# Storing the last output tile with one transfer per queue and column half instead of two

## The chip, the cores and the metric

The kernel runs on one core of a Trainium2 chip. The core has a matrix engine (PE in the profile, with PEld for its weight loads), a vector engine (DVE), a scalar engine (ACT), GpSimd (POOL) and a sync engine (SP). SP, ACT and POOL can each issue transfers to and from HBM; all of these transfers are carried out by the core's 16 DMA engines. The metric is the device time of the whole program in microseconds, as the median over runs. The median before the change is 307.31 us (three runs, 307.09 to 307.4).

## The reference

The reference computes an attention with global and local tokens and feeds its result to a two-layer network. Only the end of the second part matters here:

```python
x = attn_out.transpose(0, 2, 1, 3).reshape(B * S, H * D)   # 8 * 544 = 4352 rows of 512
h = x @ w_in                                               # 512 -> 2048
g = h * (1.0 / (1.0 + np.exp(-1.702 * h)))
return (g @ w_out).astype(np.float32)                      # 2048 -> 512
```

B is 8 (batches), S is 544 rows in each batch: Sg = 32 global rows first and 512 local rows after them. The output is 4352 rows of 512 float32 numbers, so a row is 2,048 bytes.

## The kernel before

The attention of batch i + 1 is computed between the matrix products of batch i, so that the matrix engine always has work; the order is written out by hand. The network works on nine groups of rows: group i < 8 holds the 512 local rows of batch i, and group 8 (`i == B`) holds the 256 global rows of all batches. For each group, `h_step` makes 16 slices of the hidden layer (matrix products at L495, a tanh on ACT at L502, a product on DVE at L503), and `o_mm` then multiplies them with `w_out` for one tile of 128 output rows at a time (L520). A finished tile goes to `o_out` (L525 to L542): ACT copies it out of the accumulator into the buffer `ob` and scales it by 0.5 (L534), and four transfers store it in HBM (L542), each of 32 rows.

The group of global rows comes last, and it has two tiles of 128 rows. Each of them belongs to four batches: rows 32j to 32j + 31 of a tile are the 32 global rows of one batch, so in the output the four pieces stand 544 rows apart. The very last tile (`last` in L527) is treated on its own. Its columns are cut in two halves, 0 to 319 and 320 to 511. For each of them the matrix engine runs 16 products (L532), ACT evicts the half (L534), and four transfers of 32 rows store it, two issued by SP (j = 0 and 2) and two by ACT (j = 1 and 3). So the tile ends in eight transfers. All other output tiles are stored by SP alone.

The issues of a queue are made one after the other by its engine. On SP, the store of the tile before (four of 32 rows of 512 columns) stands directly ahead of the last tile's. On ACT, the two issues of the first half stand between the eviction of the first half and that of the second. Each transfer reports its landing on one of eight semaphores that are used in turn, and the program's end, on SP, waits for all of them (L824).

Of the kernel before, what the change touches and what calls it, by code (L numbers as in the profile page):

```python
# [20 lines left out]
def kernel(  # L21
# [12 lines left out]
    nc = tc.nc  # L34

    B, H, Sl, D = q_l.shape
    Sg = q_g.shape[2]
    S = Sg + Sl
# [105 lines left out]
    for i in range(2):  # L144
# [4 lines left out]
        out=step, in_=step, pattern=[[1, 257]], compare_op=ALU.is_ge,  # L149
# [89 lines left out]
    def pbank(name):  # L239
        return psP.tile([128, 512], F32, name=name, tag="p")  # L240
# [272 lines left out]
    def o_mm(i, st):  # L513
        tci, f4 = divmod(st, 4)
        first = (i, tci) not in ops
        if first:
            ops[i, tci] = pbank("op")
        op = ops[i, tci]
        for fc in range(4 * f4, 4 * f4 + 4):
            nc.tensor.matmul(op, lhsT=gTs[i][:, fc, tci * 128 : tci * 128 + 128],  # L520
                             rhs=w_out_sb[:, fc, :], start=(first and fc == 4 * f4), stop=(fc == FC - 1))
        if f4 == 3:
            o_out(i, tci, op)

    def o_out(i, tci, op):  # L525
        ob = moe.tile([128, d_model], F32, name="ob", bufs=6)
        last = i == B and tci == B // 4 - 1  # L527
        for lo, hi in ((0, 320), (320, 512)) if last else ((0, 512),):
            if last:
                op = pbank("op")  # L530
                for fc in range(FC):
                    nc.tensor.matmul(op[:, lo:hi], lhsT=gTs[i][:, fc, tci * 128 : tci * 128 + 128],  # L532
                                     rhs=w_out_sb[:, fc, lo:hi], start=(fc == 0), stop=(fc == FC - 1))
            nc.scalar.activation(ob[:, lo:hi], op[:, lo:hi], AF.Copy, scale=0.5)  # L534
            for j in range(4):
                eng = nc.scalar if last and j % 2 else nc.sync
                if i < B:
                    rows = out[i * S + Sg : (i + 1) * S, :].rearrange("(r t) m -> t r m", t=16)[4 * tci + j]
                else:
                    r = (4 * tci + j) * S  # L540
                    rows = out[r : r + Sg, :]
                eng.dma_start(out=rows[:, lo:hi], in_=ob[32 * j : 32 * j + 32, lo:hi])  # L542
# [253 lines left out]
    for st in range(4):  # L796
        o_mm(B, st)
    o_out(B, 1, None)


# [28 lines left out]
```

## Time and profile before

| What | us |
|---|---|
| median of the runs | 307.31 |
| span of the profiled execution | 305.3 |
| PE busy in it | 298.7 (98%) |
| last matrix products (L532), start and length | 298.06, 3.66 |
| eviction of the first half (L534), start and length | 300.43, 0.44 |
| eviction of the second half (L534), start and length | 301.80, 0.33 |
| ACT's two issues of the second half, start and length together | 302.16, 0.85 |
| issue to landing of the last tile's eight stores | 1.4 to 1.7 |

The profiled execution's own time outside of its span isn't listed. The median of the runs stands 2.0 us above the span; that is what lies around the span of instructions, in so far as the profiled execution was like the others.

Times in the profile's views are counted from the first instruction of the program. A name ending in q (SPq, ACTq) is an engine's issue of a transfer or its wait; its length is the time that the engine was held by the issue, not the time of the transfer. In the view of the transfers (the DMA view) a strip of 40 digits divides the stretch asked for into equal slices; a digit is the mean busy share of the 16 DMA engines in tenths, and below it stand the GB/s that they moved. q1 is the queue that SP issues to and q10 the one that ACT issues to.

### The profile page before, as it was taken

Reading aid. Unit: us, or ns where it says so; the run is one execution under the profiler, and the core shown is the slowest. Engines: PE = TensorE matmul, PEld = TensorE weight load, DVE = VectorE, ACT = ScalarE, POOL = GpSimd, SP = SyncE. Lnnn points to the kernel's source line nnn. Section 1 sums busy time; section 2 is a strip of 40 time slices with the busy share of each in tenths; the row PEclk is TensorE's granted clock in tenths of the full one; section 3 lists DMA queues with packets and bytes.
Section 4 is the critical chain, followed back from the end, with each engine's and each line's share of the span. In section 5 each row is a group of like instructions: output and inputs, shape, how many; then the busy total and the mean of one; then the engine's idle time right before and its main releaser. Section 6 shows DMA issues by size and latency. Waiting matters only on the chain.

```text
span 305.3 us, 7862 instructions
## 1 busy us (share of the span) xinstructions
PE 298.7 (98%) x3265; PEld 148.5 (49%) x3265; DVE 211.2 (69%) x445; ACT 169.3 (55%) x282; POOL 55.7 (18%) x89
## 2 busy tenths in 40 slices
PE   7999999999999999999999999999999999999995
PEld 6454445445454455445454455445454454446653
DVE  6678858978868876777767876787677855573320
ACT  4738484585556655575457654665456661673421
POOL 8732755530050002300050002100000000000000
PEclk9999999999999999999999999999999999999999
DMA  7999999999399023941299024901130021101122
GB/s 191 178 206 207 197 180 230 211 170 131 82 112 191 10 56 84 151 97 37 54 122 170 4 56 89 101 0 48 44 86 2 2 66 48 46 0 36 36 63 75
DMA packets 56436, 29.52 MB, mean 97 GB/s; under 512 B 43088, under 2 KB 46288, under 8 KB 56400
## 3 DMA queue, kind: packets, MB, share of 16 engines
q0 software_dynamic: 46000, 16.98, 49.9%
q1 hardware_dynamic: 9920, 11.39, 14.3%
q10 hardware_dynamic: 480, 0.66, 0.7%
q8 instruction: 25, 0.41, 0.6%
q14 instruction: 11, 0.09, 0.1%
HBM read 35.13 MB, written 8.91 MB: 144 GB/s over the span
## 4 chain that ended last, share of the span: by engine, by line
PE 80%; DMA 15%; DVE 2%; POOL 1%; issue 1%; ACT 0%; ACTq 0%; DVEq 0%; POOLq 0%
PE op L520 34%; PE hp L495 33%; DMA rk<-in_k_l_dram 10%; PE s L314 5%; PE ov L426 4%; DMA rq<-in_q_l_dram 3%; DMA w_in_sb<-in_moe_w_in_dram 2%; PE ov L400 2%; DVE xL L459 1%; PE op L532 1%; PE s L444 1%; PE s L333 1%; ACTq L542 0%; ACT ob L534 0%; DVE e L354 0%
## 5 line engine op out<-in xcount | busy, mean ns | idle before, releaser
L520 PE MATMUL op<-w_out_sb,gT 128*128 128x512 bf16 x528 | 122.0, 380 | 0.0
L503 DVE SCALAR_TENSOR_TENSOR gT<-th,hp 128x512 bf16<-128x512 f32 (+1 forms) x140 | 91.2, 657 | 41.8 <-ACT th L502 40.7
L495 PE MATMUL hp<-xL,w_in_sb 128*128 128x512 bf16 x496 | 108.9, 379 | 0.3 <-DVE xL L459 0.2
L502 ACT ACTIVATE th<-hp 128x512 f32<-128x512 f32 (+1 forms) x140 | 79.9, 573 | 43.4 <-PE hp L495 39.9
L495 PEld LDWEIGHTS <-w_in_sb 128*128 128x128 bf16 x576 | 56.2, 98 | 64.7 <-issue 0.9
L520 PEld LDWEIGHTS <-gT 128*128 128x128 bf16 x528 | 49.2, 98 | 56.2 <-issue 3.5
L347 ACT ACTIVATE e<-s 128x856 bf16<-128x856 f32 x62 | 51.6, 884 | 12.1 <-PE s L444 7.0
L534 ACT ACTIVATE ob<-op 128x512 f32<-128x512 f32 (+2 forms) x35 | 20.5, 585 | 59.0 <-PE op L520 56.5
L89 POOL DMA_DIRECT2D v<-in_v_l_dram x24 | 18.7, 782 | 111.2 <-PE s L444 105.8
L450 DVE STREAM_TRANSPOSE sT<-ov 128x512 f32<-128x512 f32 x15 | 10.8, 717 | 26.9 <-PE ov L426 26.9
L354 DVE TENSOR_TENSOR e<-e,mask 128x1408 bf16<-128x1408 bf16 x28 | 24.4, 872 | 5.7 <-ACT e L347 5.7
L314 PE MATMUL s<-q,kT 32*128 32x228 bf16 (+5 forms) x528 | 21.2, 280 | 1.0 <-DVE q L275 1.0
L459 DVE TENSOR_TENSOR xL<-ov,rs 128x512 bf16<-128x512 f32 x30 | 19.3, 686 | 1.4
L314 PEld LDWEIGHTS <-kT 32*128 32x128 bf16 x528 | 10.9, 95 | 14.8 <-issue 6.6
L271 DVE STREAM_TRANSPOSE kT<-rk 128x512 f32<-128x512 f32 (+1 forms) x17 | 16.9, 994 | 1.0 <-DMA rk<-in_k_l_dram 1.0
L383 ACT ACTIVATE ek<-kb 128x512 bf16<-128x512 f32 x16 | 9.7, 608 | 9.2 <-PE kb L333 7.0
L426 PE MATMUL ov<-e,v 128*32 128x160 bf16 (+1 forms) x480 | 12.2, 239 | 0.0
L454 DVE STREAM_TRANSPOSE rs<-rT 128x512 f32<-128x512 f32 x16 | 11.4, 711 | 0.6
L275 DVE STREAM_TRANSPOSE q<-rq 128x512 f32<-128x512 f32 (+1 forms) x17 | 10.9, 641 | 1.0 <-ACT rq L558 1.0
L426 PEld LDWEIGHTS <-v 128*32 128x32 bf16 x512 | 10.0, 97 | 0.9 <-issue 0.9
L333 PE MATMUL kb<-q,kgT 32*32 32x512 bf16 x128 | 10.4, 387 | 0.0
L495 PE MATMUL hp<-xG,w_in_sb 128*128 128x256 bf16 x64 | 9.6, 273 | 0.0
(82 smaller groups left out, 170.6 us busy)
## 6 DMA issues: line engine op xcount, KB each, us to landing
out_dram<-ob SPq DMA_DIRECT2D x132, 64.0 KB, 1.7
v<-in_v_l_dram POOLq DMA_DIRECT2D x32, 128.0 KB, 6.0
rk<-in_k_l_dram POOLq DMA_DIRECT2D x6, 512.0 KB, 10.8
rq<-in_q_l_dram POOLq DMA_DIRECT2D x5, 512.0 KB, 8.6
w_out_sb<-in_moe_w_out_dram POOLq DMA_DIRECT2D x4, 512.0 KB, 10.8
rq<-in_q_l_dram POOLq DMA_DIRECT2D x5, 256.0 KB, 8.9
ek<-ek SPq DMA_DIRECT2D x13, 96.0 KB, 2.9
w_in_sb<-in_moe_w_in_dram POOLq DMA_DIRECT2D x4, 256.0 KB, 6.4
```

The lines of the kernel that those rows point to most:

```text
L89: nc.gpsimd.dma_start(out=vtiles[b % 2][p, s, :, :, :D], in_=vf[b, g][:, hs])
L271: nc.vector.transpose(self.kT.rearrange("p (r t) -> p t r", t=16)[:, lo:hi], loaded[self.b][0][:, self.u].bitcast(F32)[:, 32 * lo : 32 * hi])
L314: nc.tensor.matmul(ps[j][:, off : off + n], lhsT=self.k[p, 128 * c : 128 * c + 128, e], rhs=self.q[p, lo:hi, r0 : r0 + nr, e], start=(e == ...
L347: nc.scalar.activation(e[:, 2 * i : 2 * i + 2, :RW], self.ps[i][:, :, :RW], AF.Exp, scale=scale)
L354: nc.vector.tensor_mul(e, e, mask[:, rnd : rnd + 1, :].to_broadcast([128, 4, LW]))
L426: nc.tensor.matmul(ov[32 * j : 32 * j + 32, :].rearrange("p (t r) -> p t r", t=16)[:, :, r0 : r0 + nr], lhsT=lv, rhs=self.E[c // 2][:, j, ...
L459: nc.vector.tensor_mul(self.x[:, 2 * self.u + h, :], self.st[1 + h], self.st["rs"])
L495: nc.tensor.matmul(hp[:, : width(i)], lhsT=w_in_c[:, fc // 8, kc, fc % 8 // 2, :, fc % 2], rhs=(xL[i] if i < B else xG)[:, kc, :], start=( ...
L502: nc.scalar.activation(th[:, :n], hp[:, :n], AF.Tanh, scale=0.851)
L503: nc.vector.scalar_tensor_tensor(gTs[i][:, fc, :n], in0=th[:, :n], scalar=1.0, in1=hp[:, :n], op0=ALU.add, op1=ALU.mult)
L520: nc.tensor.matmul(op, lhsT=gTs[i][:, fc, tci * 128 : tci * 128 + 128], rhs=w_out_sb[:, fc, :], start=(first and fc == 4 * f4), stop=(fc = ...
L534: nc.scalar.activation(ob[:, lo:hi], op[:, lo:hi], AF.Copy, scale=0.5)
```

## The change

For the last tile alone, the loop over four pieces is replaced by one over two pairs of pieces. Each store now takes 64 partitions of `ob` and writes them to 2 blocks of 32 rows in HBM, 544 rows apart. SP issues the one for the first two blocks, ACT the one for the last two. The tile ends in four transfers instead of eight, and the amount of data is the same. All other tiles are stored as before.

```diff
             nc.scalar.activation(ob[:, lo:hi], op[:, lo:hi], AF.Copy, scale=0.5)
+            if last:
+                rows = out.rearrange("(b s) m -> b s m", s=S)[4:8, :Sg, lo:hi]
+                for k, eng in enumerate((nc.sync, nc.scalar)):
+                    eng.dma_start(out=rows[2 * k : 2 * k + 2], in_=ob[64 * k : 64 * k + 64, lo:hi])
+                continue
             for j in range(4):
-                eng = nc.scalar if last and j % 2 else nc.sync
+                eng = nc.sync
                 if i < B:
```

In the built program, the patterns of the transfers are these (step and count of each dimension in elements, outermost first, for the first half):

```
before   on chip [512, 32] [1, 320]            in HBM [512, 32] [1, 320]
after    on chip [512, 64] [1, 1] [1, 320]     in HBM [278528, 2] [512, 32] [1, 320]
```

No other instruction is added, removed or moved on any engine.

## The prediction

> **What bounds the kernel now.** I read the page first, for the engine that is full, then the order of events in the last 8 us, because everything that the change touches comes after the last matrix product.
>
> ```profile
> span 305.3 us, 7862 instructions
> PE 298.7 (98%) x3265; PEld 148.5 (49%) x3265; DVE 211.2 (69%) x445; ACT 169.3 (55%) x282; POOL 55.7 (18%) x89
> ```
>
> The matrix engine is busy for 298.7 of 305.3 us. A change of the last stores cannot alter those; it can only alter the tail behind them. The view of instructions in order of time shows that tail:
>
> ```profile
> 298.06 3.66 PE L532 MATMUL op<-w_out_sb,gT 128*128 128x320 bf16 x32
> ...
> 298.88 4.05 SPq L542 DMA_DIRECT2D out_dram<-ob  x8
> 300.43 0.44 ACT L534 ACTIVATE ob<-op 128x320 f32<-128x320 f32 x1 [1.58 <-PE op L532]
> 300.90 0.85 ACTq L542 DMA_DIRECT2D out_dram<-ob  x2
> 301.80 0.33 ACT L534 ACTIVATE ob<-op 128x192 f32<-128x192 f32 x1 [0.93 <-PE op L532]
> 302.16 0.85 ACTq L542 DMA_DIRECT2D out_dram<-ob  x2
> ```
>
> The products end at 301.72 (298.06 + 3.66), the second eviction at 302.13, and then two issues on each queue follow, until 303.01 on ACT. Nothing but the transfers runs after that. How long they take, the view of transfers between 302.9 and 303.9 shows, which are those of the second half alone:
>
> ```profile
> DMA  0006248694694321100004338369676352100000
> DMA packets 192, 0.10 MB, mean 99 GB/s; under 512 B 64, under 2 KB 192, under 8 KB 192
> q10 hardware_dynamic: 96, 0.05, 18.4%
> q1 hardware_dynamic: 96, 0.05, 18.3%
> ```
>
> A digit is 25 ns here. Data run from the fourth slice (302.97) to 303.80, in two humps: the first issue of each queue, then the second. The 192 packets are 128 of data (4 stores of 32 rows, one packet of 768 bytes each) and 64 of under 512 bytes, 16 for each store: every store is dealt out to all 16 engines, two rows for each, and each engine closes its share with a small packet. This dealing is what the forecast turns on. From 303.80 to the end of the span, 305.34, come the landing, SP's closing waits and the end of the program: 1.54 us that the change leaves as they are.
>
> **The change part by part.** The sum is made against the span of 305.3 us; the profiled execution's own full time isn't listed, and the median of the runs, 307.31, stands 2.0 us above the span. I add the difference of the spans to the median.
>
> *Removed: one issue on each queue in each half.* One row prices an issue before the change (the line of the stores, from 300.7 on):
>
> ```profile
> L542 SPq DMA_DIRECT2D out_dram<-ob x4: 314/318/427, 300.9 to 302.6; - x4
> L542 ACTq DMA_DIRECT2D out_dram<-ob x4: 375/405/434, 300.9 to 302.6; - x4
> ```
>
> In the first half, an issue removed on ACT (0.43) frees ACT at about 301.3 instead of 301.75. The next eviction starts at 301.80 and waits for the products, which end at 301.72, so this is worth at most 0.05 us; I take nothing, since matrix work covers it. In the second half the removed issue is the last one of each queue; it stands 0.42 us behind the first on ACT (302.16 to 302.57), so up to 0.4 us of the tail goes with it, if the transfer that is left is as fast. SP's last issue also waits until 302.61 for a semaphore that ACT's first store held; that wait goes too and is worth nothing alone, since ACT's last packets are later than SP's. Nothing else is queued behind these issues: on both queues the program ends there.
>
> *Added to the issues that stay: a pattern with one more dimension.* No store before has it. Nearest below are the stores of the same tile, 314 to 434 ns. Nearest above are copies on chip that SP issues, of another kind:
>
> ```profile
> L100 SPq DMA_DIRECT2D ek<-ek x13: 522/528/538, 40.0 to 246.3; - x13
> ```
>
> So an issue costs 0.1 us less to 0.2 more than now; I take 0.11 more (528 against 419 to 434, the longer of a pair), because the pattern is the less simple one. The first data then start at 301.82 instead of 301.71.
>
> *Changed: how a transfer is dealt to the engines.* A store before has 32 rows as its outermost dimension on both sides, and its rows are dealt out in 16 shares. The new one has 64 on chip and 2 in HBM, and 32 rows below that. The trace has no transfer with an outermost dimension under 32, so it bounds this cost only from both sides: 16 engines, with 4 rows for each, or, if the dealing goes by the outermost dimension that both sides share, 2 engines with 32 rows each. The rate of one engine is bounded by two rows. Above by a stretch in which the engines are full, 3.6 to 4.4 us:
>
> ```profile
> DMA packets 173, 0.32 MB, mean 397 GB/s; under 512 B 18, under 2 KB 18, under 8 KB 173
> q1 hardware_dynamic: 99, 0.19, 67.1%
> q10 hardware_dynamic: 74, 0.12, 40.4%
> ```
>
> That is 397 / 16 = 24.8 GB/s for one engine. Below by the stretch of the second half: 98,304 bytes in 36.7% of 16 engines' 1 us, that is 16.7 GB/s while an engine is busy; there all 16 engines draw on the same 32 partitions.
>
> With two engines, and both queues on the same two, each has to move half of the tile, 131,072 bytes: 5.28 us at 24.8 GB/s, 7.85 us at 16.7. The second half (issued at 302.15) queues behind the first, so the engines never idle in between. The last packet ends at 301.82 + 5.28 = 307.10 instead of 303.80: 3.3 us later. I take the upper rate, because few engines with long runs of rows are more like the full stretch than like 16 that collide; the lower one gives 309.67, 5.9 us later. With 16 engines, see the rivals.
>
> I take two engines. What the rows show is that rows are dealt, and that they are dealt along the outermost dimension is the simplest reading of two rows for each of 16 engines; a dimension of 2 has two shares.
>
> The sum: issues of the first half 0; issue of the new form +0.11; dealing and rate +3.19 (5.28 us of transfer in place of the 2.09 from 301.71 to 303.80); wait on SP 0; together +3.3 us. 307.31 + 3.3 = 310.6 us.
>
> **What the notes on the chip say.** The Trainium skill, "DMA: Bandwidth & Descriptors", section "Why a DMA increments its semaphore by 16 and not by 1", says that a transfer runs on the largest number of engines up to 16 that divides the slowest dimension of more than one element on both sides, and that transfers issued from SP or ACT use the lowest-numbered ones. The 16 closing packets of each 32-row store agree with it; no transfer in this trace shows a smaller number. By it the new stores, with 64 and 2, run on two engines, and SP's and ACT's on the same two. Against it stands the same page's section "Rules for kernel authors", where many small transfers are to be merged into a large one; taken alone, that rule would give 307.0 to 307.1, as in the rival of 16 engines. The page's "Specifications" give about 27 GiB/s (29 GB/s) for an engine; as an estimate, 131,072 bytes would then take 4.5 us, and the time would be 309.8 us.
>
> **The rivals.**
>
> *Sixteen engines (not slower).* If the pattern is dealt by rows, or by the on-chip side's 64, a store keeps all engines. The second half's data start at 302.97 + 0.11 = 303.08 on SP and up to 303.2 on ACT, and 98,304 bytes take 0.25 us at 397 GB/s to 0.37 at 16.7 for each engine: they end at 303.5 to 303.6 instead of 303.80. The time would be 307.0 to 307.1. For it: the rows of both sides lie evenly, and nothing in the trace forbids it. Against it: an outermost dimension of 2. It decides from about 8 engines on: 98,304 bytes on N engines at 24.8 GB/s take 3.96 / N us, and 303.27 (the later issue price) + 3.96 / N meets 303.80 at N = 7.5.
>
> *A pair of engines for each queue.* Then four engines work, each with 65,536 bytes, 2.64 us: 301.82 + 2.64 = 304.46, 0.7 later, 308.0 us. For it: q1 and q10 are separate queues. Against it: in the full stretch both queues' shares add up to 107.5% of the same 16 engines.
>
> *One engine.* If the middle dimension of 1 on chip or the 2 spoils the dealing altogether: 262,144 bytes at 24.8 GB/s are 10.57 us, until 312.39, 8.6 later, 315.9 us. Against it: the two blocks have an even share each.
>
> **How the numbers follow.** A measurement of this kernel can tell about 0.2%, 0.6 us, from no change. Two shared engines 0.77, a pair for each queue 0.06, one engine 0.04, sixteen (or eight) 0.13. The range starts at the four-engine case, 308.0, and ends at two engines at the lower rate, 307.31 + 5.9 = 313.2; it leaves out sixteen engines and one, some 0.17, and a little above. Sixteen engines gain 0.2 to 0.3 us, which is within 0.2%; only with issues as cheap as now, and data to match, would they gain over 0.6. So faster 0.02, same 0.12, slower 0.86.
>
> **What would show it.** In the changed kernel, the issues of L538 take about 0.53 us each; the four stores land 4.5 to 5.6 us after issue instead of 1.4 to 1.7; the strip of busy DMA engines stands at 1 (two of 16) from 302 to 307, with some 50 GB/s; there are 2 small closing packets for each store, not 16; the products and evictions before 302.13 stay as they are. The forecast is wrong if the stores still land within 2 us: then the dealing is by rows. If they land at about 2.5 us, four engines work; if the strip stays at 1 but for 8 us, the rate of one engine was taken too high.

## The result, and the profile after

The change makes the kernel slower. The median is 312.15 us (six runs, 311.73 to 312.33) against 307.36 us before, measured beside it; the ratio is 1.0146, with a 95% interval of 1.0109 to 1.0182. The forecast was 310.6 us with a range of 308.0 to 313.2: right in sign and in how the stores are dealt to the engines, 1.5 us too low in size.

The view of instructions in order of time, of the changed kernel (start, length in us, engine, line):

```profile
298.22 3.66 PE L532 MATMUL op<-w_out_sb,gT 128*128 128x320 bf16 x32
...
300.60 0.44 ACT L534 ACTIVATE ob<-op 128x320 f32<-128x320 f32 x1 [1.58 <-PE op L532]
301.06 2.32 SPq L538 DMA_DIRECT2D out_dram<-ob  x2
301.06 1.38 ACTq L538 DMA_DIRECT2D out_dram<-ob  x1
302.49 0.33 ACT L534 ACTIVATE ob<-op 128x192 f32<-128x192 f32 x1 [1.46 <-PE op L532]
302.85 0.52 ACTq L538 DMA_DIRECT2D out_dram<-ob  x1
```

The last products end at 301.88 (298.22 + 3.66) and the span at 310.53. In different profiled executions of kernels that are the same up to there, the products end anywhere from 301.2 to 302.5 us, so below I compare tails, from the end of the last product to the end of the span. The tail was 3.62 us before (301.72 to 305.34) and is now 8.65: 5.0 us more, which covers the 4.8 us by which the medians differ. Two lines have changed ahead of the transfers: ACT's first issue holds ACT for 1.38 us, and the second eviction starts 0.61 us behind the products instead of 0.08.

What follows the issues is in the view of transfers over the stretch of the last tile's data, 302.3 to 309.1 us (a digit is 0.17 us; the view counts a packet's whole time in the slice in which it starts):

```profile
DMA  1201011121020111111111111111111111111110
GB/s 23 23 0 15 23 38 45 30 30 15 8 45 8 45 45 45 45 53 53 45 45 53 53 45 45 60 39 45 45 50 50 45 45 45 45 50 50 45 45 9
DMA packets 264, 0.26 MB, mean 39 GB/s; under 512 B 8, under 2 KB 264, under 8 KB 264
```

The 264 packets are 256 rows and 8 small closing packets: two for each of the four stores, where there were 16 for each before. The busy share is 1 tenth of the 16 engines, and the rate mostly 45 to 53 GB/s once it is steady, where the last four stores before moved 99 GB/s on average in the view of the prediction. So each store is carried by two engines, and both queues share the same two. The trace also shows two phases, and the same view cuts them apart (302.3 to 304.8, then 304.9 to 309.0):

```profile
DMA  0200220020200111111201401300001301001121
...
DMA packets 50, 0.06 MB, mean 26 GB/s; under 512 B 0, under 2 KB 50, under 8 KB 50
...
q1 hardware_dynamic: 50, 0.06, 12.4%
```

```profile
DMA  1111111111111111111111111111111111111111
...
DMA packets 210, 0.19 MB, mean 47 GB/s; under 512 B 8, under 2 KB 210, under 8 KB 210
```

In the first 2.5 us the two engines move 26 GB/s, both together, and only SP's rows: in the packet records, ACT's first row starts at 304.89, 3.8 us after ACT's first issue. The engines are not idle in this stretch, although the strip has zeros. SP's packets take 12.4% of the time of 16 engines, and two engines are 12.5%; a zero stands where a long packet from an earlier slice is still running. What is slow is single rows: in the packet records, 13 of SP's first 52 rows took 89 to 419 ns, the others 53 to 67. (The texts below that were written before the runs call these stretches "gaps".)

From 304.89 on, every row of 1,280 bytes takes 55 ns and every one of 768 takes 36, and each engine starts one every 52 or 33 ns. The queues take turns while both have rows to move. SP's second store, though issued at 302.85, starts only at 306.82, when ACT's first has one row left to start.

### The profile page after: what moved, and what is told of

The parts are those of the page before. It is cut to its first block, busy times and chain, and to the rows that moved or that the text cites. A ratio compares the mean times of both kernels' runs of the same rounds, so it can differ in the third digit from the quotient of the medians.

```text
span 310.5 us, 7858 instructions
## 1 busy us (share of the span) xinstructions
PE 298.9 (96%) x3265; PEld 148.4 (48%) x3265; DVE 210.7 (68%) x445; ACT 169.3 (55%) x282; POOL 55.7 (18%) x89
## 4 chain that ended last, share of the span: by engine, by line
PE 78%; DMA 14%; DVE 2%; POOL 1%; issue 1%; ACT 0%; ACTq 0%; DVEq 0%; POOLq 0%
PE op L520 33%; PE hp L495 33%; DMA rk<-in_k_l_dram 9%; PE s L314 5%; PE ov L426 4%; DMA rq<-in_q_l_dram 3%; DMA w_in_sb<-in_moe_w_in_dram 2%; PE ov L400 2%; DVE xL L459 1%; PE op L532 1%; PE s L444 1%; PE s L333 1%; ACTq L538 0%; ACT ob L534 0%; DVE e L354 0%
```

## The experiments

The theory is that of the prediction: a store is dealt out along its outermost dimension, and 2 blocks as that dimension leave two engines. The rivals are that the form of the store (64 rows, three dimensions, blocks far apart) makes it slow by itself, that the issues do, or that one queue can't hand out rows faster. The table has all runs; the tail is taken from each run's profile, "closing packets" is the count in the stretch of the last tile's data over the number of its stores (in the last two rows, that of the two new stores). The cuts of code are against the changed kernel where nothing else is said, and "..." marks lines left out.

| Run | median, us | before beside it | ratio (95%) | tail, us | closing packets per store |
|---|---|---|---|---|---|
| before | 307.36 | | | 3.62 | 16 |
| changed kernel | 312.15 | 307.36 | 1.0146 (1.0109 to 1.0182) | 8.65 | 2 |
| rows outermost | 307.52 | 307.43 | 1.0009 (0.9975 to 1.0042) | 3.71 | 16 |
| four blocks, one store per half | 309.66 | 307.43 | 1.007 (1.0047 to 1.0094) | 5.78 | 4 |
| all four stores on SP | 312.45 | 307.43 | 1.0151 (1.0106 to 1.0196) | 8.83 | 2 |
| rows outermost, one store per half | 307.32 | 307.43 | 0.9992 (0.9971 to 1.0013) | 3.68 | 16 |
| before, with the long issue | 309.13 | 307.51 | 1.0068 (1.0047 to 1.009) | 4.72 | 16 |
| new stores in the second half only | 310.59 | 307.51 | 1.0112 (1.0093 to 1.013) | 5.76 | 2 |
| new stores in the first half only | 310.75 | 307.51 | 1.0109 (1.0092 to 1.0127) | 7.01 | 2 |

### The same stores with the rows outermost

The global rows of the last four batches are placed in another order on chip, so that partitions hold row 0 of two batches, then row 1 of both, and so on. The store then has the 32 rows as its outermost dimension in HBM and the 2 blocks inside. Nothing else differs from the changed kernel: four stores, two on each queue, 64 rows, three dimensions, the same bytes.

```diff
+    def at(b):
+        if b < 4:
+            return xG[:, :, Sg * b : Sg * b + Sg]
+        k, r = divmod(b - 4, 2)
+        return xG[:, :, 128 + 2 * Sg * k : 128 + 2 * Sg * (k + 1)].rearrange("p c (s b) -> p c b s", b=2)[:, :, r]
...
-                xG[:, 2 * self.u : 2 * self.u + 2, Sg * self.b : Sg * self.b + Sg],
+                at(self.b)[:, 2 * self.u : 2 * self.u + 2, :],
...
-                rows = out.rearrange("(b s) m -> b s m", s=S)[4:8, :Sg, lo:hi]
+                rows = out.rearrange("(b s) m -> s b m", s=S)[:Sg, 4:8, lo:hi]
                 for k, eng in enumerate((nc.sync, nc.scalar)):
-                    eng.dma_start(out=rows[2 * k : 2 * k + 2], in_=ob[64 * k : 64 * k + 64, lo:hi])
+                    eng.dma_start(out=rows[:, 2 * k : 2 * k + 2], in_=ob[64 * k : 64 * k + 64, lo:hi])
```

> The rows of the last tile are put in another order on chip (row 0 of two batches, row 1 of both, and so on), so that each 64-row store has the 32 rows as its outermost dimension in HBM and the 2 blocks inside it. The number of stores, their queues, the number of rows, the row lengths and the number of dimensions are those of the changed kernel. Dealing by the outermost dimension: 16 closing packets for each store instead of 2, landing within 2.3 us of issue, and a time of 307.0 to 308.0 us (up to 0.7 of it for ACT's first issue of 1.38 us, if that stays). Rival, that the third dimension or the two far blocks make the store slow by themselves: landing stays at 6 us and the time at 312.

The view of transfers over this run's last stores, 302.9 to 304.9 us:

```profile
DMA  0054949799399995210000000476786487741000
...
DMA packets 320, 0.26 MB, mean 131 GB/s; under 512 B 64, under 2 KB 320, under 8 KB 320
```

There are 64 closing packets, 16 for each store; the engines are busy to nine tenths and the two halves are two short humps. The stores land 1.9 to 2.5 us after issue (I had expected 2.3 at most), and the time is 307.52 us and cannot be told from before. With the order of two dimensions in one pattern, 5 us come and go: the form, the number of rows and the distance of the blocks are not the cause, the dealing is.

### Four blocks as the outermost dimension

One store of 128 rows for each half, all on SP.

```diff
-                for k, eng in enumerate((nc.sync, nc.scalar)):
-                    eng.dma_start(out=rows[2 * k : 2 * k + 2], in_=ob[64 * k : 64 * k + 64, lo:hi])
+                nc.sync.dma_start(out=rows, in_=ob[:, lo:hi])
```

> Each half of the last tile is stored by one transfer of 128 rows, issued by SP alone, with 4 blocks as the outermost dimension in HBM. Dealing by the outermost dimension: 4 closing packets for each store; each engine has 32 rows of either half, some 52 and 33 ns each as in the changed kernel, 2.7 us in all from 302.3 on, so that data end near 305.1 instead of 309.0 and the time is 308.1 to 308.8 us. Rival, that the rate is limited by what one queue can hand out, whatever the number of engines: 128 rows on one queue take at least as long as 64 on each of two, 312 us or more.

The view of transfers, 302.8 to 306.8 us:

```profile
DMA  0233023012222222232223222222222222210000
...
DMA packets 264, 0.26 MB, mean 66 GB/s; under 512 B 8, under 2 KB 264, under 8 KB 264
```

Eight closing packets for two stores are four each, the strip stands at 2 tenths, and the rate in the steady part is about 90 GB/s, twice that of the changed kernel. The count of engines follows the outermost dimension: 2, 4, 16. One queue alone does better than two did, so a limit of one queue is out. The time, 309.66 us, lies 0.9 us above the end of what was expected; data took 3.8 us instead of 2.7, and the slow rows are there again (22 of the first half's 128 took 81 to 334 ns in the packet records).

### All four stores on SP

```diff
-                for k, eng in enumerate((nc.sync, nc.scalar)):
+                for k, eng in enumerate((nc.sync, nc.sync)):
```

> All four 64-row stores of the changed kernel are issued by SP, none by ACT. If both queues share the same two engines, the transfers need the same 5.4 us; ACT's 1.38 us issue is gone, so the second eviction is back at 0.1 us behind the matrix products. If the gaps between packets (302.4 to 304.6 in the changed kernel) come from two queues being served at once, data end at 302.3 + 5.4 = 307.7 and the time is 310.8 to 311.1 us; if they come from the form of the store alone, it stays at 312. A pair of engines for each queue would make it 2.7 us slower than the changed kernel, some 314.8.

The view of transfers, 302.5 to 309.6 us, and the second eviction in order of time:

```profile
DMA  1201011110201111102001111111111111111100
...
q1 hardware_dynamic: 264, 0.26, 12.6%
```

```profile
298.41 3.66 PE L532 MATMUL op<-w_out_sb,gT 128*128 128x320 bf16 x32
...
302.11 0.33 ACT L534 ACTIVATE ob<-op 128x192 f32<-128x192 f32 x1 [0.88 <-PE op L532]
```

The eviction is back at 0.04 us behind the products (298.41 + 3.66 = 302.07), and the tail is 8.83 us all the same. So ACT's long issue in the changed kernel cost nothing: there, rows of the second half start 4.0 us after their issue, at 306.82, since the two engines had more than enough rows ahead of them. Here two engines are busy throughout (12.6% of 16), and the slow rows are there too: 18 of the first half's 128 took 84 to 359 ns, the last of them until 306.18. So they do not come from two queues being served at once; my better case (310.8 to 311.1) was wrong, the other one (312) right. A pair of engines for each queue, which would have made this run 2.7 us slower than the changed kernel, is out: it took 312.45 us against 312.15.

### The issues: the stores of before with the long form of issue

In the built programs, a flag that lets the compiler use a short form of issue stands at the stores with two dimensions, and at none with three. This run takes it from the eight stores of the last tile and leaves the rest of the kernel before as it was (the cut is against that kernel).

```diff
+            if last:
+                nc.dge_precook = False
             for j in range(4):
                 eng = nc.scalar if last and j % 2 else nc.sync
```

> The kernel before, with all eight stores of the last tile as they were (32 rows, two dimensions, 16 engines); only the flag that lets the compiler use the short form of issue for such stores is taken away for them, as it is for every store with three dimensions. If the issue form costs what the runs with the rows outermost show (0.64 us held instead of 0.31 to 0.43, data 1.22 us after the issue starts instead of 0.82), the second issue of the second half starts 0.2 us later and its data another 0.4 us later: the time from the last matrix product to the end grows from 3.63 to 4.1 to 4.3 us and the median to 307.9 to 308.1. Rival, that the third dimension or the 64 rows made those issues slow and the flag nothing: 3.6 us and 307.4.

The stores' line (lengths in ns), and ACT in order of time:

```profile
L544 SPq DMA_DIRECT2D out_dram<-ob x4: 508/567/589, 301.5 to 303.9; - x4
L544 ACTq DMA_DIRECT2D out_dram<-ob x4: 518/704/858, 301.5 to 303.9; - x4
```

```profile
301.50 1.45 ACTq L544 DMA_DIRECT2D out_dram<-ob  x2
302.99 0.33 ACT L534 ACTIVATE ob<-op 128x192 f32<-128x192 f32 x1 [1.52 <-PE op L532]
303.35 1.42 ACTq L544 DMA_DIRECT2D out_dram<-ob  x2
```

An issue holds its engine for 0.51 to 0.86 us instead of 0.31 to 0.43, and the first data start 1.20 us after it instead of 0.82. Two of them in a row on ACT take 1.45 us, which now outlasts the products and puts the second eviction 0.67 us behind them. The tail grows by 1.1 us and the median by 1.6; I had expected 0.5 to 0.7. This also says what merging is worth: with the long form, eight stores need 309.13 us and four (rows outermost) 307.52. The merge gains and the long issue that comes with a third dimension takes it back, so that nothing is left against before.

### One store for each half, rows outermost

As in the first run (the cut is against it), with all four batches interleaved, so that one store of 128 rows does for a half, the first on SP and the second on ACT.

```diff
-                for k, eng in enumerate((nc.sync, nc.scalar)):
-                    eng.dma_start(out=rows[:, 2 * k : 2 * k + 2], in_=ob[64 * k : 64 * k + 64, lo:hi])
+                (nc.scalar if lo else nc.sync).dma_start(out=rows, in_=ob[:, lo:hi])
```

> As the run with the rows outermost, but with all four blocks inside: one store of 128 rows for each half, the first issued by SP, the second by ACT, each with 32 rows as the outermost dimension in HBM. Dealing by the outermost dimension: 16 closing packets for each of two stores; each engine has 8 rows of 1,280 and 8 of 768 bytes, 0.42 and 0.27 us at the full rate; data of the second half start 1 to 1.3 us after its issue at 302.15 and end at 303.6 to 304.1 (before: 303.80). Time 307.0 to 307.7 us. Rival, that a store costs by its number of blocks: slower than 312.

The view of transfers, 301.6 to 303.5 us:

```profile
DMA  0037989998983200000000000000589899630000
...
DMA packets 288, 0.26 MB, mean 138 GB/s; under 512 B 32, under 2 KB 288, under 8 KB 288
```

Sixteen closing packets for each of two stores, two clean humps, no issue left that anything waits for: 307.32 us, ratio 0.9992. It is the best that merging reaches here, and it can't be told from the kernel before: the second half's data start 1.31 us after their issue, where the first of the short issues needs 0.82 and the second stands 0.42 behind it, 1.24 in all.

### One half at a time, and the slow rows at the start

Two runs keep the new stores in one column half only and store the other half as before, in stores that go to all 16 engines. They ask whether the slow rows belong to the start of such a store, to the first write to a stretch of HBM, or to two such stores in a queue. The cut is that for the second half only; for the first half only the condition is `if last and not lo:`.

```diff
-            if last:
+            if last and lo:
...
-                eng = nc.sync
+                eng = nc.scalar if last and j % 2 else nc.sync
```

> The first column half is stored as before (eight-way dealing untouched: four stores of 32 rows), only the second half by the two new stores of 64 rows. Two engines: 98,304 bytes, 64 rows of 768 bytes for each at 33 to 36 ns, 2.1 to 2.3 us, from 303.4 on; data end at 305.6 instead of 303.8, the time is 309.0 to 309.3 us. If the gaps between packets seen in the changed kernel belong to the start of such a store, whatever it writes, another 1 us is added here: 310.0 to 310.4. If they belong to the first write to a stretch of HBM rows (the first half has written to these rows before), there are none.

The view of transfers for the second half only, 304.1 to 305.3 and then 305.4 to 306.8 us:

```profile
DMA  0000201202031000111001120010110023000100
...
DMA packets 42, 0.03 MB, mean 27 GB/s; under 512 B 0, under 2 KB 42, under 8 KB 42
```

```profile
DMA  0310011111111111121111111111111111112111
...
DMA packets 81, 0.06 MB, mean 43 GB/s; under 512 B 2, under 2 KB 81, under 8 KB 81
```

The slow rows are there although the first half had been written to the same rows of HBM before, so the first write is out. The stretch is shorter, 1.4 us until the last of them ends: 12 of SP's 64 rows took 64 to 169 ns. Up to ACT's first row, 43 rows took 27 ns each for the two engines together, where the steady part has 16.5; that is 0.4 us lost, not the 1 us expected. The median, 310.59 us, is a little above the case with gaps, but the tail of the profiled execution is 2.1 us above that of before, which would make 309.6; I have no account of the rest. (The granted clock was 0.997 and 0.995 in the runs of 309.94 and 310.15 us, 0.991 and 0.990 in those of 311.12 and 311.03; whether that is the rest isn't shown.)

> Only the first column half is stored by the two new stores, the second half by four stores of 32 rows as before. Two engines move 64 rows of 1,280 bytes each, 3.3 us from 302.3 on, and 1.2 us more if the gaps come from the start or the first write; the second half's shares on the same two engines queue behind them (2 rows for each of 4 stores, 0.3 us), while its shares on the other 14 engines are long done. Data end at 306.0 without gaps, 307.2 with them; the time is 309.5 or 310.7 us. If the gaps come from two stores of this kind standing in one queue, there are none here. ACT's first issue tells whether its 1.38 us belongs to the first store of this kind on ACT (it stays) or to a second one waiting (it is 0.5 to 0.7).

ACT in order of time, for the first half only:

```profile
301.21 1.39 ACTq L538 DMA_DIRECT2D out_dram<-ob  x1
302.64 0.33 ACT L534 ACTIVATE ob<-op 128x192 f32<-128x192 f32 x1 [1.46 <-PE op L532]
```

The time, 310.75 us, is that of the case with gaps (310.7): data of the first half go on until 307.1 in the packet records, and the second half's stores of 32 rows, issued at 303.0, finish only at 307.3. Of each one's 16 landings, 14 came by 306.3 and the last two from 307.2 on: two of the 16 engines that each is dealt to are still busy. A second store of the new kind in a queue isn't needed for the slow rows: 13 of the 64 of SP's store took 91 to 367 ns. And it isn't only its own rows that are slow: of the second half's rows, which go to all 16 engines, the first 30 start before 305.0, and 29 of them took 107 to 331 ns, where the longest before the change took 64.

ACT's first issue stays at 1.39 us here (1.29 in the run before this one), against 0.52 for the second one in the changed kernel and 0.64 with the rows outermost; so it belongs to the first two-engine store on ACT, next to SP's. Why it does isn't shown.

What makes these rows slow stays open. Shown is that it needs neither two queues, nor two stores in a queue, nor a first write, and that it ends: in the changed kernel only rows of SP's first store are slow, and all that come later take 55 or 36 ns. It doesn't go by the number of rows stored: from the first row to the end of the last slow one it lasts 2.2 us in the changed kernel and 2.2 with the first half only, which has half the rows, 1.4 with the second half only and 3.7 with all stores on SP. Whether it lies in how the rows are handed out to the engines, no run shows.

## Why the prediction was right, and where it was off

**What bounds the kernel, and that only the tail moves.** Right: PE is as busy as before (298.9 us against 298.7), and the tail alone accounts for the difference.

**How a transfer is dealt.** Right, and this step carries the result. Two closing packets per store, a strip at 1 tenth, some 50 GB/s, as stated beforehand; four with an outermost dimension of 4, and 16 with the rows outermost. The section of the Trainium skill's page "DMA: Bandwidth & Descriptors" that the prediction weighed ("Why a DMA increments its semaphore by 16 and not by 1") agrees with 2, 4 and 16 here. The same page's rule of merging small transfers did not decide: merged on 16 engines they gain nothing in the end, merged on two they lose.

**Both queues on the same two engines.** Right: the packets of both queues alternate on two engines, and all stores on SP take as long.

**The transfer's length, 5.28 us.** This is the term of the sum that was mis-sized. Data run from 302.34 to 309.0 in the packet records, 6.7 us. The rate itself was nearly right: in the steady part 47 GB/s, 23.5 for an engine, against 24.8; 64 rows at 52 ns and 64 at 33 are 5.44 us. What was missing is the start: the first 2.55 us moved 52 rows, 49 ns each instead of 26, which is 1.2 us lost. The prediction said that the engines never idle in between, and this held, since two engines are busy throughout (12.4% of 16). It took the full rate from the first row on, and that failed: 13 rows took 89 to 419 ns. The prediction's other estimate, 309.8 us at 29 GB/s for an engine, was further off.

**The issue of the new form, +0.11 us.** Too low. An issue holds for 0.52 to 0.67 us (ACT's first 1.38), near the 0.53 that was named, but I counted the holding alone. The first data start 1.28 us after the issue instead of 0.82, so this term is 0.45. The run with the long issue shows it for the stores of before as well.

**Issues of the first half, 0.** Right for the wrong reason. I took it that ACT would be free earlier and that the products would cover it. ACT was held longer and the eviction came 0.6 us later; it cost nothing because the two engines were behind by more than that, as the run with all stores on SP shows. The prediction's sign that the evictions before 302.13 stay as they are was wrong for the same reason.

Taken together, 0.45 + 4.6 (6.7 of data in place of 2.1) is the 5.0 us of the tail, against 0.11 + 3.19 in the forecast. The landing times that the prediction named, 4.5 to 5.6 us, were 4.9 for SP's first store, 6.2 for ACT's first and 6.5 to 6.6 for the last two, by the last landing of each on its semaphore.

**The rival of 16 engines** would not have been 0.2 to 0.3 us faster, as I priced it, but even: the run that has it shows a tail 0.1 us longer than before, since the long issue eats the gain.

## What to carry to other kernels

Before two stores are merged, look at the outermost dimension of both sides of the merged pattern, and count the small closing packets in the view of transfers: here they were the number of engines that carried a store. Where blocks are to be merged, order the rows on chip so that they interleave the blocks, and the long dimension can stand outermost; here its 32 rows kept all 16 engines. Look also at what a third dimension does to the issue, because what merging saves in issues can be lost in the longer start of each.

## What was not expected of the hardware

- A store with the long form of issue starts its data 1.2 to 1.3 us after the issue, one with the short form 0.82; eight of them made the kernel 1.6 us slower (309.13 us).
- The first two-engine store starts slowly, at 26 to 27 GB/s for both engines instead of 43 to 47: 12 or 13 of its 64 rows take up to 419 ns instead of 55 (or 169 instead of 36), over 1.4 to 2.2 us, and with two such stores on one queue over 3.7. No row took over 127 ns with the rows outermost, or 108 before the change.
- With such a store issued by SP and by ACT at the same time, ACT's issue took 1.29 to 1.39 us the first time, and ACT's rows began 2.4 to 3.8 us after it (3.8 in the changed kernel), when 43 to 54 of SP's 64 had started.
